# A fused attention, MoE and MoE kernel: seven block products in three quarters of the first MoE, one list planner for all work behind the attention, token operands in DRAM

## The chip, the cores and the metric

The kernel runs on one core of one Trainium2 chip. The metric is device time in microseconds (us) for one execution. A core has a TensorE (PE) that multiplies, a VectorE (DVE), a ScalarE (ACT) and a GpSimd (POOL) for everything else, and a SyncE (SP) whose queue issues the transfers. Each engine works through its own list of instructions in the order in which they were written, and waits at semaphores for the others. Matmuls write to PSUM, which has eight banks of 512 fp32 values per partition.

## The reference

```python
attn_out = _attn_ref(q, k, v)                     # 4 x 8 heads, 576 positions, banded masks
x = attn_out.transpose(0, 2, 1, 3).reshape(2304, 512)
# first MoE: d_ff = 2048
h = x @ w_in
g = np.maximum(h, 0.0) + alpha * np.minimum(h, 0.0)
x = g @ w_out
# second MoE: 8 experts of 1024, weighted by P (8 rounds of row and column normalising)
P = sinkhorn(x @ w_gate)
for e in range(8):
    out += P[:, e:e + 1] * (np.maximum(x @ w1[e], 0.0) @ w2[e])
```

## The kernel before, in words

Every product is computed from two fp32r parts of each operand, a high part and the rest: three matmuls (high x high, high x rest, rest x high) for each 128-row tile, written by the helper `three` (L362). So each operand must be split first: ACT copies the high part, and DVE or POOL subtracts it.

The program has three stages.

**Attention** (L164 to L353). Sixteen groups, each a pair of heads of one of four batches, go through five steps: scores `att_S`, exponentials `att_E`, sums `att_R`, transposes `att_X`, values `att_V`. `att_V` (L245) leaves 288 tokens at a time in `XS`, as the two parts (`xh`, `xl`). Between these steps stand units of the first MoE.

**First MoE.** A unit is a chunk of 288 tokens (eight of them, `NCH`) times a slice of 256 hidden columns (eight, `st`). `m1_L1` (L367) multiplies by `w_in`, applies the leaky relu and splits the result; `m1_L2` (L397) multiplies by `w_out` and adds to the accumulator `acc` of the chunk, on DVE (L413) or, for the first slice, by a copy on ACT (L411). The 64 units are written one behind another, the second layer of a unit merged with the first layer of the next (`run`, L578). Beside them `Side` objects hand out small pieces of other work at a rate set by a due step: the conversion of the weights, which come as 64-bit words and are turned into fp32 parts by `from_double` (L507, five instructions on DVE, then ACT and POOL), the attention (`aside`), the gate (`gside`), and the conversion of four w1 weight sets of the second MoE ahead of time (`pside`, `convert_ahead`, L642).

**Second MoE.** 768 tokens at a time (three blocks), sixteen half experts each, so 48 passes. Both layers use seven products of quarter blocks in place of eight (`PRODUCTS`, L733): sums of the blocks of both operands are formed first, and the results are put together from the seven products. In the first block some passes (`EIGHTH`, six of sixteen) use the plain eight products in the second layer. The order of all this work is made by a list planner, `arrange` (L804): each operation has a cost per engine and a due time, and at each step the engine that is free first takes its most urgent ready operation. The tail of the first MoE (`close_m1`, L949) goes through the planner as well.

PSUM in the second MoE: `W01` and `X01` of two banks each for the first layer, and `SW0`, `SW1`, `SX0`, `SX1` for the second.

Of the kernel before, what the change touches and what calls it, by code (L numbers as in the profile page):

```python
# [43 lines left out]
PRE = 4  # L44
EIGHTH = (0, 1, 4, 7, 10, 13)
# [14 lines left out]
def program(tc, qk, v, moe_w_in, moe_w_out, moe_alpha, moe2_w_gate, moe2_w1, moe2_w2, masks, out):  # L60
# [7 lines left out]
    spill = pool(es, "spill", space=bass.MemoryType.DRAM)  # L68
    py = pool(sp, "py", bufs=2, space=PSUM)
# [15 lines left out]
    gp = pool(sr, "gp", bufs=2, side="right")  # L85
    accp = pool(sr, "accp", side="right")
    attc = pool(sa, "attc", side="right")
# [4 lines left out]
    accs = [None] * 3 + [accp] * 3 + [None] * 2  # L92
# [9 lines left out]
    eye = attc.tile([P, P], BF16, name="eye")  # L102

# [141 lines left out]
    def att_V(i):  # L245
# [6 lines left out]
        for g in range(2):  # L252
            pv = bank("psV")
            for j in range(g * (NB // 2), NB // 2 + 1 + g * (NB // 2)):
                lo, hi = max(j * QB, g * CH), min((j + 1) * QB, (g + 1) * CH)
                for hh in range(2):
# [6 lines left out]
                    )  # L263
            if p < 2:
                c = 2 * b + g
                nc.scalar.copy(xh(c, p), pv[:, :CH])
                low_part(nc.vector, xl(c, p), pv[:, :CH], xh(c, p))
                continue
            for cc in range(2):
# [5 lines left out]
                low_part(nc.vector, lo, src, ho)  # L275

# [83 lines left out]
    below = [None]  # L360
# [6 lines left out]
    def m1_L1(n, c, st):  # L367
        ah, al = wa_of[n]
        for t in range(FS // P):
# [7 lines left out]
            gh = gp.tile([P, CH], F32R, tag="gh", name="gh", bufs=4)  # L377
            gl = gp.tile([P, CH], F32R, tag="gl", name="gl", bufs=4)
            u = gp.tile([P, CH], F32, tag="u", name="u")
            if below[0] is None:  # L380
                nc.vector.tensor_scalar(
                    out=u, in0=ps[:, :CH], scalar1=0.0, scalar2=alpha[:, ft : ft + 1], op0=ALU.min, op1=ALU.mult
                )
                nc.vector.scalar_tensor_tensor(out=u, in0=ps[:, :CH], scalar=0.0, in1=u, op0=ALU.max, op1=ALU.add)
            else:
                neg = below[0].tile([P, CH], F32, tag="neg", name="neg")
                nc.scalar.activation(neg, ps[:, :CH], AF.Relu, scale=-1.0)  # L387
                nc.vector.scalar_tensor_tensor(  # L388
                    out=u, in0=neg, scalar=rest[:, ft : ft + 1], in1=ps[:, :CH], op0=ALU.mult, op1=ALU.add
                )  # L390
# [56 lines left out]
    for st in order[2:-2]:  # L447
        add_units(inst_of(("a", st)), st, range(NCH), order)
    ends = [inst_of(("a", st)) for st in order[-2:]]
    for cs in ((0, 1), (2,), (3,), (4,), (5,), (6,), (7,)):  # L450
        for inst, st in zip(ends, order[-2:]):
            add_units(inst, st, cs, order)
# [1260 lines left out]
```

## Time and profile before

| | |
|---|---|
| median of 3 runs | 1971.38 us (1966.68 to 1973.65) |
| the profiled execution | 1972.87 us, its span 1971.1 us |
| PE busy | 1940.9 us, 98% of the span |
| DVE, ACT, POOL busy | 71%, 47%, 33% |
| granted TensorE clock, mean | 0.995 |
| moved by DMA | 408.34 MB, mean 207 GB/s |
| share of PE in the chain that ended last | 94% |

How to read it: a busy share is of the whole span, and a matmul's own duration contains its way through the array, so neighbouring matmuls overlap. What a matmul costs in a row of them is the distance from start to start. In the page's 40 slices PE stands at 9 (90% or more) in all but the first, and the clock in all of them. The times of the stages, from the trace: the first unit of the first MoE starts at 39.9 us, the last attention group ends in the unit that starts at 155.0, the second MoE's first product starts at 521.05.

### The profile page before, as it was taken

The page shows a single profiled execution, that of the slowest core. Times are in us where ns is not written, and L with a number is a line of the kernel's source. Part 1 is how long each engine was busy: PE and PEld are TensorE (multiplying, and loading weights), DVE is VectorE, ACT ScalarE, POOL GpSimd, SP SyncE. Part 2 cuts the span into 40 slices and gives each one's busy share as a digit, 9 for nine tenths or more (in the row PEclk, how much of TensorE's full clock was granted, in tenths as well). Part 3 has the DMA queues.
Part 4 walks back from the last instruction along what each step waited for, and adds up shares of the span by engine and source line. Part 5 has one row for each costly group of instructions (what it writes and reads, how often), then busy time and mean ns, then how long its engine had stood idle before and what let it go on. Part 6 is the DMA issues. An engine that isn't in the chain of part 4 may idle for free.

```text
span 1971.1 us, 37433 instructions
## 1 busy us (share of the span) xinstructions
PE 1940.9 (98%) x14755; PEld 1919.9 (97%) x14755; DVE 1409.0 (71%) x2302; ACT 928.4 (47%) x1740; POOL 644.2 (33%) x569
## 2 busy tenths in 40 slices
PE   6999999999999999999999999999999999999999
PEld 5889999999999999999999999999999999999998
DVE  6765776764458888777786777777776777777776
ACT  6654444434445555555545444444444443443442
POOL 4434666645235464545422332120200100100100
PEclk9999999999999999999999999999999999999999
DMA  7422343320457777666786886757687666766762
GB/s 236 142 76 70 115 144 121 131 86 29 141 177 256 277 260 278 233 218 248 262 342 233 310 304 216 254 195 241 231 307 274 237 217 215 240 214 215 242 212 86
DMA packets 126607, 408.34 MB, mean 207 GB/s; under 512 B 13024, under 2 KB 41440, under 8 KB 122080
## 3 DMA queue, kind: packets, MB, share of 16 engines
q1 hardware_dynamic: 126432, 405.95, 59.5%
q8 instruction: 116, 1.90, 0.4%
q14 instruction: 59, 0.48, 0.1%
HBM read 294.76 MB, written 111.15 MB: 206 GB/s over the span
## 4 chain that ended last, share of the span: by engine, by line
PE 94%; DMA 2%; DVE 1%; issue 1%; POOL 1%; ACT 1%; SPq 0%; POOLq 0%; DVEq 0%; ACTq 0%
PE SW L365 7%; PE SW L363 7%; PE SW L364 7%; PE W L363 7%; PE W L364 7%; PE W L365 7%; PE SX L365 6%; PE SX L364 5%; PE SX L363 5%; PE X L363 5%; PE X L364 5%; PE X L365 5%; PE psH L363 3%; PE psH L365 3%; PE psH L364 3%; PE psY L363 3%
## 5 line engine op out<-in xcount | busy, mean ns | idle before, releaser
L1499 DVE SCALAR_TENSOR_TENSOR oR<-SW,pt,oR 128x256 f32<-128x256 f32 x372 | 174.3, 480 | 125.4 <-PE SW L365 120.9
L363 PE MATMUL W<-XS,WT 128*128 128x384 f32 x768 | 258.4, 336 | 0.0
L364 PE MATMUL W<-XS,WT 128*128 128x384 f32 x768 | 257.8, 336 | 0.0
L365 PE MATMUL W<-XS,WT 128*128 128x384 f32 x768 | 257.6, 335 | 0.0
L1499 DVE SCALAR_TENSOR_TENSOR oR<-SX,pt,oR 128x256 f32<-128x256 f32 x360 | 171.9, 480 | 87.4 <-PE SX L365 86.9
L363 PE MATMUL X<-XS,WT 128*128 128x384 f32 x576 | 194.4, 338 | 2.8 <-ACT X L1343 2.8
L364 PE MATMUL X<-XS,WT 128*128 128x384 f32 x576 | 193.9, 337 | 0.0
L365 PE MATMUL X<-XS,WT 128*128 128x384 f32 x576 | 193.8, 337 | 0.0
L599 POOL TENSOR_TENSOR WT<-RAW,WT 128x512 fp32r<-128x512 f32 (+1 forms) x75 | 98.7, 1325 | 270.7 <-ACT WT L1167 136.8
L392 POOL TENSOR_TENSOR gl<-u,gh 128x288 fp32r<-128x288 f32 x126 | 104.1, 826 | 178.5 <-ACT gh L391 174.0
L364 PE MATMUL psH<-XS,WT 128*128 128x288 f32 x504 | 149.2, 296 | 1.3 <-DVE XS L143 1.3
L363 PE MATMUL psH<-XS,WT 128*128 128x288 f32 x504 | 150.3, 298 | 0.1
L365 PE MATMUL psH<-XS,WT 128*128 128x288 f32 x504 | 149.4, 296 | 0.0
L599 POOL TENSOR_TENSOR wR<-rawR,wR 128x512 fp32r<-128x512 f32 x38 | 51.0, 1342 | 300.3 <-ACT wR L1167 145.2
L363 PEld LDWEIGHTS W<-XS,WT 128*128 128x128 f32 x768 | 144.7, 188 | 0.2
L364 PEld LDWEIGHTS W<-XS,WT 128*128 128x128 f32 x768 | 144.4, 188 | 0.0
L365 PEld LDWEIGHTS W<-XS,WT 128*128 128x128 f32 x768 | 144.1, 188 | 0.0
L599 DVE TENSOR_TENSOR hR<-WX,hR 128x768 fp32r<-128x768 f32 x127 | 142.2, 1124 | 0.6 <-ACT hR L1289 0.3
L388 DVE SCALAR_TENSOR_TENSOR u<-neg,rest,psH 128x288 f32<-128x288 f32 x108 | 55.4, 513 | 114.0 <-ACT neg L387 107.4
L1289 ACT CAST hR<-WX 128x768 fp32r<-128x768 f32 x128 | 105.4, 835 | 65.0 <-DVE WX L1365 60.6
L599 POOL TENSOR_TENSOR WT<-rawR,WT 128x512 fp32r<-128x512 f32 (+1 forms) x47 | 63.5, 1357 | 168.4 <-ACT WT L1167 73.6
L363 PE MATMUL psY<-gh,WT 128*128 128x288 f32 x376 | 113.2, 301 | 1.0 <-ACT acc L411 1.0
(275 smaller groups left out, 6509.4 us busy)
## 6 DMA issues: line engine op xcount, KB each, us to landing
RAW<-in_moe_w SPq DMA_DIRECT2D x19, 1024.0 KB, 6.7
WT<-a11g SPq DMA_DIRECT2D x36, 512.0 KB, 4.4
WT<-S2g SPq DMA_DIRECT2D x36, 512.0 KB, 4.4
WT<-a12g SPq DMA_DIRECT2D x36, 512.0 KB, 3.6
WT<-S3g SPq DMA_DIRECT2D x36, 512.0 KB, 3.7
WT<-S1g SPq DMA_DIRECT2D x36, 512.0 KB, 3.6
WT<-a22g SPq DMA_DIRECT2D x36, 512.0 KB, 4.6
WT<-S4g SPq DMA_DIRECT2D x36, 512.0 KB, 4.0
```

Source lines behind the costliest of these rows:

```text
L363: nc.tensor.matmul(ps, lh, rh, start=start, stop=False, skip_group_check=more)
L364: nc.tensor.matmul(ps, lh, rl, start=False, stop=False, skip_group_check=more)
L365: nc.tensor.matmul(ps, ll, rh, start=False, stop=stop, skip_group_check=more)
L388: nc.vector.scalar_tensor_tensor(out=u, in0=neg, scalar=rest[:, ft : ft + 1], in1=ps[:, :CH], op0=ALU.mult, op1=ALU.add)
L392: nc.gpsimd.tensor_tensor(out=gl, in0=u, in1=f(gh), op=ALU.subtract)
L599: eng.tensor_tensor(out=out, in0=x, in1=y, op=op)
L1289: add(act(n2), lambda _: nc.scalar.copy(hv(h[n])[:, 0], tm[i]), prio, [("t", i)], [(h[n], "h")])
L1499: nc.vector.scalar_tensor_tensor(out=o, in0=x, scalar=p_, in1=o, op0=ALU.mult, op1=ALU.add)
```

## The change

**First MoE.** Only the first two slices (`st` 0 and 1, a quarter of d_ff) keep the plain form. The other six are taken as three blocks of 512 hidden columns, and each block is computed for one batch (576 tokens) at a time: twelve passes. Their first layer uses the seven products; the second layer stays plain, twelve matmuls for each output tile. The leaky relu works on 576 columns at once (`leaky`).

**Accumulators.** In the new second layer each output tile is seeded: ACT copies the accumulator into the PSUM bank before the matmuls add to it, and copies the sum back after them. DVE's additions of L413 are gone there.

**Token operands.** `att_V` also copies each value tile, unsplit, to `xst`, and SP stores it to DRAM (`x32`). From there `m1_tokens` loads a batch, forms the four sums on DVE or POOL, splits them and stores them to DRAM (`xm`). Later passes load their operands from there.

**Weights.** Eight pieces of the first new block's weights are converted during the attention stage (`early`) and stored to DRAM (`wd`); the other sixteen are converted between the new passes (`double`).

**Planner.** From the tenth unit on (the first one on chunk 6) everything is ordered by `arrange`: seven plain units, twelve new passes, 48 passes of the second MoE. A place in SBUF now has a plan of uses by era. Of w1 only one set is converted ahead (`AHEAD`), and the first block has seven passes with eight second-layer products: `EIGHTH` is (0, 1, 2, 5, 8, 11, 14).

```diff
-PRE = 4
-EIGHTH = (0, 1, 4, 7, 10, 13)
+EIGHTH = (0, 1, 2, 5, 8, 11, 14)
...
+    x32 = [spill.tile([P, KD, 2 * CH], F32, name=f"x32b{b}") for b in range(B)]
...
+            if g == 0:
+                whole = xst[:, i % 2]
             if p < 2:
                 c = 2 * b + g
                 nc.scalar.copy(xh(c, p), pv[:, :CH])
+                nc.scalar.copy(whole[:, g * CH : (g + 1) * CH], pv[:, :CH])
                 low_part(nc.vector, xl(c, p), pv[:, :CH], xh(c, p))
+                if g:
+                    nc.sync.dma_start(x32[b][:, p], whole)
                 continue
...
+    def early(i):
+        load_raw(piece_at[2, i])
+        yield from from_double(raw_of.pop((2, i)), None, None, wd[i])
+        load_raw(piece_at[2, i] + 2)
...
+        if far is not None:
+            nc.gpsimd.tensor_tensor(out=ab, in0=t, in1=lw, op=ALU.add)
+            nc.sync.dma_start(far, ab)
+            return
...
+        def m1_layer1(v):
+            fi = 1 + v // B
...
+            for i, (a, xn, bk) in enumerate(PRODUCTS):
+                ps = WX01[bk]
...
+                        for k in range(2):
+                            three(ps[:, st, :CH], wv[:, 0, k, st], wv[:, 1, k, st], x[:, 0, k], x[:, 1, k], first and k == 0, k == 1, True)
...
+        def m1_layer2(v):
...
+            for cc in range(2):
+                c = 2 * b + cc
+                for d in range(KD):
+                    K, bk = next_bank(4 if v < B else 3)
...
+                    if seeded:
+                        add(act(CH), lambda _, c=c, d=d, bk=bk: nc.scalar.copy(bk[:, :CH], acc[c][:, d]), t - 1, [A], [K])
+                    add([("PE", 1.59)], mm, t, reads, [K])
+                    if seeded:
+                        add(act(CH, True), lambda _, c=c, d=d, bk=bk: nc.scalar.copy(acc[c][:, d], bk[:, :CH]), t + 1.2, [K], [A])
...
-        for i, u in enumerate(units[:-1]):
+        hand = next(i for i, u in enumerate(units) if u[2] == NCH - 2)
+        EARLY_AT = 4
+        for i, u in enumerate(units[:hand]):
+            if i == EARLY_AT:
+                for j in range(EARLY):
+                    wside.add(early(j), 5, begin[hand - 1])
...
+        second(prev, units[hand:])
```

**Matmuls.** Up to the start of the tenth unit PE's list is the same in both kernels, row for row. Over the whole program it has 3136 matmuls of 288 columns before and 2992 after, 6156 of 256 columns before and 6174 after, and as many of every other width.

**DVE, from the second hidden values of the eighth unit on** (`u`, `GU`: hidden values; `XS`: values of the attention; L531 before and L522 to L536 now: steps of a weight conversion). Before:

```order
L381 TENSOR_SCALAR u<-psH,alpha 128x288
L384 SCALAR_TENSOR_TENSOR u<-psH,u 128x288
L143 TENSOR_TENSOR XS<-psV,XS 128x2x72 x8
L531 SCALAR_TENSOR_TENSOR RAW<-RAW 128x512
L381 TENSOR_SCALAR u<-psH,alpha 128x288
L384 SCALAR_TENSOR_TENSOR u<-psH,u 128x288
L413 TENSOR_TENSOR acc_96<-psY,acc_96 128x288
```

Now:

```order
L396 TENSOR_SCALAR GU<-psH,alpha 128x288
L399 SCALAR_TENSOR_TENSOR GU<-psH,GU 128x288
L146 TENSOR_TENSOR XS<-psV,XS 128x2x72 x4
L532 TENSOR_SCALAR RAW<-WX 128x512
L536 SCALAR_TENSOR_TENSOR RAW<-RAW 128x512
L522 TENSOR_SCALAR WX<-RAW 128x512
L146 TENSOR_TENSOR XS<-psV,XS 128x2x72 x4
L526 SCALAR_TENSOR_TENSOR WX<-RAW,WX 128x512
L530 SCALAR_TENSOR_TENSOR WX<-WX 128x512
L532 TENSOR_SCALAR RAW<-WX 128x512
L536 SCALAR_TENSOR_TENSOR RAW<-RAW 128x512
L522 TENSOR_SCALAR WX<-RAW 128x512
```

The first hidden values of the ninth unit, the fifth row before, now come four rows behind the last one shown (the rest of the conversion that it begins). One step of a conversion stood ahead of them; now the last two steps of one and two whole ones do. From the fifth unit's second hidden values to this place the list now holds eight conversions, before parts of two.

**SP, the same stretch** (`RAW`: two buffers for weight words; `wd`: converted pieces). Before:

```order
L476 DMA RAW<-in_moe_w_in 128x1024
L129 DMA v<-in_v 96x1152
L476 DMA RAW<-in_moe_w_in 128x1024
L129 DMA v<-in_v 96x1152 x2
L648 DMA praw<-in_moe_w 128x4x256
L660 DMA a11g_2358<-pboth 256x1x256
L476 DMA RAW<-in_moe_w_out 128x1024
```

Now:

```order
L542 DMA wd_108<-WX 128x512
L485 DMA RAW<-in_moe_w_out 128x1024
L275 DMA x32b_63<-xst 128x576
L287 DMA x32b_63<-xst 128x576
L132 DMA v<-in_v 96x1152
L542 DMA wd_109<-WX 128x512
L485 DMA RAW<-in_moe_w_out 128x1024
L542 DMA wd_110<-WX 128x512
L485 DMA RAW<-in_moe_w_out 128x1024
L287 DMA x32b_63<-xst 128x576 x2
L542 DMA wd_111<-WX 128x512
```

Each load into a RAW buffer stands behind the store of a converted piece and behind the stores of the tokens, which wait for ACT.

**ACT, first MoE in its steady part.** Before:

```order
L537 CAST WT<-WX 128x512
L654 CAST pboth<-praw 128x256
L387 ACTIVATE neg<-psH 128x288
L391 CAST gh<-u 128x288
L517 ACTIVATE WX<-RAW 128x512
```

Now:

```order
L1284 ACTIVATE WX<-X_2340 128x576
L1358 COPY acc_102<-SX_2343 128x288
L1355 COPY SX_2343<-acc_102 128x288
L1286 CAST XS<-WX 128x576 x2
L1284 ACTIVATE WX<-W_2339 128x576
L1358 COPY acc_102<-SX_2344 128x288
```

Each bank of the second layer (`SX`, `SW`) is now copied back and seeded again by two neighbouring rows, between the copies of the first layer.

## Rows read from the trace of the kernel before

**Rows 1.** The page, part 1: busy time, share of the span, instructions

```profile
PE 1940.9 (98%) x14755; PEld 1919.9 (97%) x14755; DVE 1409.0 (71%) x2302; ACT 928.4 (47%) x1740; POOL 644.2 (33%) x569
```

**Rows 2.** Busy us by stretch: PE, PEld, DVE, ACT, POOL; clock; DMA; GB/s

```profile
300.00:350.00 50.00, 50.00 (x379) 50.00 (x378) 34.66 (x71) 21.01 (x51) 34.04 (x41) 1.00 0.37 121
600.00:650.00 50.00, 50.00 (x362) 49.93 (x362) 40.61 (x64) 28.25 (x44) 24.39 (x18) 1.00 0.73 259
```

**Rows 3.** Timeline of PE: start, duration, instruction; seven rows between

```profile
1100.05 0.29 PE L363 MATMUL SX<-WT,hR 128*128 128x256 f32 x1
...
1101.01 0.28 PE L365 MATMUL SW<-wR,hR 128*128 128x256 f32 x1
```

**Rows 4.** The same, two stretches of the attention stage

```profile
39.90:77.40 37.50, 32.47 (x460) 28.38 (x458) 25.95 (x56) 25.54 (x93) 16.33 (x13) 0.95 0.41 126
115.10:155.00 39.90, 35.30 (x382) 32.65 (x379) 23.98 (x54) 20.12 (x57) 12.36 (x12) 0.91 0.24 74
```

**Rows 5.** Timeline of DVE, two instructions, others between

```profile
112.94 1.12 DVE L197 TENSOR_REDUCE mx<-psS 128x5 f32<-128x480 f32 x2 [0.57 <-PE psS L186]
...
156.90 0.52 DVE L381 TENSOR_SCALAR u<-psH,alpha 128x288 f32<-128x288 f32 x1 [1.39 <-PE psH L365]
```

**Rows 6.** Groups by line, a weight conversion: busy us, mean ns, idle before

```profile
L518 DVE TENSOR_SCALAR WX<-RAW 128x512 uint32<-128x512 uint32 x7 | 3.2, 459 | 6.9 <-DMA RAW<-in_moe_w_in 6.9
L522 DVE SCALAR_TENSOR_TENSOR WX<-RAW,WX 128x512 uint32<-128x512 uint32 x7 | 4.8, 679 | 0.1
L525 DVE SCALAR_TENSOR_TENSOR WX<-WX 128x512 f32<-128x512 f32 x9 | 9.1, 1015 | 0.9
L527 DVE TENSOR_SCALAR RAW<-WX 128x512 uint32<-128x512 uint32 x7 | 2.9, 421 | 0.1
L531 DVE SCALAR_TENSOR_TENSOR RAW<-RAW 128x512 f32<-128x512 uint32 x7 | 5.0, 721 | 0.1
L542 POOL TENSOR_TENSOR WX<-WX,WT 128x512 f32<-128x512 f32 x9 | 12.9, 1428 | 19.9 <-DVE RAW L527 11.0 <-ACT WT L529 6.6 <-DVE rest L113 2.3
```

**Rows 7.** DMA issues, us to landing: 0 to 170, then 100 to 161

```profile
RAW<-in_moe_w_in SPq DMA_DIRECT2D x6, 512.0 KB, 5.3
...
RAW<-in_moe_w_in SPq DMA_DIRECT2D x2, 512.0 KB, 3.2
```

**Rows 8.** Timelines of DVE and of POOL, one instruction each

```profile
100.73 1.94 DVE L525 SCALAR_TENSOR_TENSOR WX<-WX 128x512 f32<-128x512 f32 x1
...
100.16 1.96 POOL L222 TENSOR_TENSOR s<-s,rs 128x864 f32<-128x864 f32 x1 [1.76 <-DVE rs L221]
```

**Rows 9.** Groups by line on ACT

```profile
L411 ACT COPY acc<-psY 128x288 f32<-128x288 f32 x32 | 13.0, 418 | 2.4 <-PE psY L365 2.4
L391 ACT CAST gh<-u 128x288 fp32r<-128x288 f32 x126 | 54.6, 434 | 111.4 <-DVE u L388 77.9 <-DVE u L384 31.9 <-POOL s L222 1.6
L1343 ACT COPY X<-W 128x768 f32<-128x768 f32 x48 | 37.6, 784 | 17.1 <-PE W L365 16.9
L595 ACT CAST gxh<-acc 128x576 fp32r<-128x576 f32 x12 | 7.8, 669 | 0.0
L1167 ACT CAST WT<-RAW 128x512 fp32r<-128x512 f32 x103 | 62.3, 620 | 47.0 <-DMA RAW<-in_moe_w 13.4 <-PE W L364 12.5 <-PE SW L365 3.6
```

**Rows 10.** The hand-over to the second MoE: busy time by stretch and PE's waits

```profile
515.00:540.00 25.00, 22.42 (x142) 21.55 (x141) 10.44 (x18) 10.37 (x19) 2.84 (x3) 0.93 0.64 224
...
PE X L363 <- ACT X L1343: 2.6, 1, 2.6
```

**Rows 11.** Groups by line on DVE in the second MoE

```profile
L599 DVE TENSOR_TENSOR hR<-WX,hR 128x768 fp32r<-128x768 f32 x127 | 142.2, 1124 | 0.6 <-ACT hR L1289 0.3
L1365 DVE SCALAR_TENSOR_TENSOR WX<-W,WX 128x768 f32<-128x768 f32 x84 | 76.4, 951 | 19.1 <-PE W L365 19.1
L1499 DVE SCALAR_TENSOR_TENSOR oR<-SW,pt,oR 128x256 f32<-128x256 f32 x372 | 174.3, 480 | 125.4 <-PE SW L365 120.9 <-issue 1.9 <-DMA out<-oR 0.9
L1424 DVE SCALAR_TENSOR_TENSOR oR<-SX,pt,oR 128x512 f32<-128x512 f32 x12 | 9.0, 748 | 2.8 <-PE SX L365 2.5
```

More of the change, by code (lines that the diff above doesn't have):

```diff
@@ L376, in m1_L1 @@
             ft = st * (FS // P) + t
[L377 to L390, printed above, removed]
+            k = made[0]
+            made[0] += 1
+            gh, gl = gview(k % 4)
+            u = GU[:, k % 2]
+            nc.vector.tensor_scalar(
+                out=u, in0=ps[:, :CH], scalar1=0.0, scalar2=alpha[:, ft : ft + 1], op0=ALU.min, op1=ALU.mult
+            )
+            nc.vector.scalar_tensor_tensor(out=u, in0=ps[:, :CH], scalar=0.0, in1=u, op0=ALU.max, op1=ALU.add)
             nc.scalar.copy(gh, u)
@@ L670, in program @@
-    lgs = {}
-    gate_split = set()
-    def gate(c, parts):
-        flush()
-        ps = bank("psG")
-        gate_mm(ps, parts)
-        gate_out(c, ps)
-    def gate_mm(ps, parts):
-        for kk in range(KD):
-            for i in range(2):
-                nc.tensor.matmul(
-                    ps[: 2 * E, :CH],
-                    wg[:, kk],
-                    parts[kk // 2][i][:, kk % 2],
-                    start=(kk == 0 and i == 0),
-                    stop=(kk == KD - 1 and i == 1),
-                )
@@ L807, in add @@
         return o
+    arranging = []
     def arrange(places, more):
-        free = {c: list(v) for c, v in places.items()}
+        free = {c: [] for c in queue_of}
         heads = {c: 0 for c in queue_of}
@@ L817, in arrange @@
         wire = [0.0]
+        BACKLOG, FAR = 5.0, 30.0
         done = []
@@ L856, in arrange @@
                 continue
-            lead = max(o.engines.values()) + (5.1 if "SP" in o.engines else 0.1)
+            cost = max(o.engines.values())
+            lead = cost * 1 + 0.1 + (5 if "SP" in o.engines else 0)
             o.prio = min(x.prio for x in o.next) - lead
-        for c in queue_of:
-            bind(c)
+        for place in places:
+            admit(place, 0.0)
         while len(done) < len(ops):
@@ L869, in arrange @@
             t, e = best
-            o = min((o for o in lists[e] if at(o, e) <= t), key=lambda o: (o.prio, o.seq))
+            o = min((o for o in lists[e] if at(o, e) <= t), key=lambda o: (o.prio + (5 if e == "DVE" and "POOL" in o.engines else 0), o.seq))
+            if e == "SP" and wire[0] > t + BACKLOG and o.prio > t + FAR:
+                o.ready = wire[0] - BACKLOG
+                continue
             cost = o.engines[e]
@@ L883, in arrange @@
             done.append(o)
-            for c, ats in more.get(o, {}).items():
-                free[c] += [(end, at) for at in ats]
-                bind(c)
+            for place in more.get(o, ()):
+                admit(place, end)
             late = end + (0.25 if e == "PE" else 0.1)
@@ new lines, in second, with release @@
+        g_done = joined_many(4, lambda: g_next)
+        g_next = [right_place(words_of(GP, 4 * CH * j, 4 * CH), [("h", 2), ("w2", NF - 1)]) for j in range(2)]
+        g_places = [Place(lambda k=k: gview(k), [("g", ALL)], g_done) for k in range(4)]
+        places += g_places[2:]
+        d_done = joined(2, Place(words_of(RAW, 0, 2048), [("raw", ALL)]))
+        places += [Place(words_of(RAW, 1024 * i, 1024), [("dbl", ALL)], d_done) for i in range(2)]
+        def release(keys, prio, freed):
+            add([("PE", 0.0)], lambda _: None, prio, (), keys)
+            later_places[ops[-1]] = freed
@@ L1132, in weights @@
             b = got[m, u] = {}
-            full = (m == 1 or g >= PRE) and sb_ == (m if plain2(g) else 0)
+            full = (m == 1 or not any(g in x for x in AHEAD.values())) and sb_ == (m if plain2(g) else 0)
             plain, sums = PLAIN[m], {s[0]: s[1:] for s in SUMS[m]}
```

977 lines of the change are left out of this document (658 added, 319 removed).

## The prediction

> **What bounds the kernel now.** First the page's busy times: PE 98% of the span, DVE 71%, ACT 47%, POOL 33% [rows 1]. A busy PE may still be a slow one, so second the busy time by stretch, with the number of matmuls. In a steady stretch of the first MoE PE is busy 50.00 of 50 us, the clock is full, and 379 matmuls of 288 columns take 50 us: 0.132 us each, start to start. In the second MoE it is busy 50.00 of 50 as well [rows 2], and there a row of eight 256-column matmuls takes 0.96 us, 0.120 each [rows 3]. So behind the attention PE is bound by the number of its matmuls, and a matmul less is worth its distance in full. In the attention stage this is not so: from 39.9 to 77.4 PE is busy 32.47 of 37.5 us, from 115.1 to 155.0 it is busy 35.30 of 39.9 with a clock of 0.91, and there PE waits for chains through the other engines [rows 4]. A change that takes matmuls out of the later part and puts DVE and ACT work into the attention stage therefore has to be weighed in two places.
>
> **Step 1: the matmuls.** A new pass has 7 x 12 = 84 matmuls in its first layer where eight products would have 96: 12 less, in 12 passes 144, as the two lists say (3136 - 2992). 144 x 0.132 = 19.0 us less [rows 2]. One more pass of the second MoE has eight products in its second layer: 18 matmuls of 256 columns more, 18 x 0.120 = 2.2 us [rows 3]. Both stand on PE's own list, which is full there, so nothing of them is hidden: -16.8 us.
>
> **Step 2: eight early conversions on DVE.** One conversion is five DVE instructions of 459, 679, 1015, 421 and 721 ns, 3.3 us, and a POOL addition of 1.43 us [rows 6]. The eight must be through before the ninth unit's first hidden values, which DVE takes up at 156.90 now; the list before them begins at the maxima of 112.94 [rows 5]. So the stretch is 44.0 us long. DVE works 23.98 of 39.9 us in its middle [rows 4]; without the parts of two conversions in it, about 6 us, some 18 are left, and with the ends of the stretch some 20. The conversion ahead of it is also finished earlier in the new list, which puts 2.7 us more in front. 20 + 2.7 + 8 x 3.3 = 49 us of DVE work for 44 us: at best 5 us late. Worse, there are only two RAW buffers: a conversion's buffer is refilled when POOL has read it (1.43), and the load takes 3.2 to 5.3 us to land [rows 7]; with some 0.5 us for hand-overs a buffer is back 5.1 to 7.2 us after its conversion. The other buffer's conversion with its share of other work takes 3.3 + 20/8 = 5.8. At 5.3 us a pair costs 5.8 + 7.2 = 13.0, and as the first two pieces are there already, eight cost 3 x 13.0 + 11.6 = 50.6, with the 2.7 us in front 53.3 us for 44: 9.4 late. And DVE cannot be full: of the 15.9 us that it is idle there, some are waits for PE and ACT that stay. I take 10 us, a little over the slow landing. The ends: 5 us if it packs perfectly; 26 us if nothing of 8 x 3.3 finds an idle place. What is behind: the second layer of the eighth unit and the first planned unit need the PSUM banks that DVE empties, so PE waits for all of it.
>
> **Step 3: 32 copies on ACT and their stores.** A 288-column copy from PSUM takes 418 ns [rows 9], 32 x 0.418 = 13.4 us. From 77 to 115 us PE is full and hides them; from 115 on they are beside the DVE queue of step 2. Where they can show is the early stretch, in which PE has 5.0 us of waits and ACT is busy 25.54 of 37.5 [rows 4]: eight copies, 3.3 us at most, 0 at least. I take 1.5. SP issues 16 stores among the loads; a store waits for ACT's copy, and the next `v` and `qk` loads behind it with it, which is in the same bound.
>
> **Step 4: the new passes themselves.** PE needs 180 x 0.132 = 23.8 us for one. ACT's own work in a pass: three copies and four relus of 576 columns from PSUM (between 418 for 288 and 784 for 768, so 0.62 us), four casts of 669, eight seeds (no such row; nearest 434, a copy of 288 out of SBUF) and eight copies back of 418 [rows 9]: 4.3 + 2.7 + 3.5 + 3.3 = 13.8 us. From ACT's list 37 weight casts of 620, 25 token and gate casts of 669, 16 first conversion steps of about as much and a few others fall into these twelve passes: 58 us, 4.8 a pass. That is 18.6 of 23.8 us, 78%. An engine so full beside a full PE is not new here: DVE is busy 40.61 of 50 us while PE misses nothing [rows 2], and that is the same planner. I take 0. Its cover is the other two second-layer banks; what it costs without cover is the slow rival below. Seeds could be dearer than their nearest row; at 784 ns each, the row for 768 columns, they add 2.8 us to a pass and it still fits (21.4). The store and reload of the tokens adds transfers to a stretch in which DMA is busy 0.37 [rows 2]; the second MoE's stretch runs at 0.73 with a full PE, so I take 0 for these too.
>
> **Step 5: the hand-overs.** Before, PE waits 2.6 us for one ACT copy at the start of the second MoE, and the clock over these 25 us is 0.93 of full, so 7% or 1.7 us are lost to the half level after this stop [rows 10]: 4.3 us. Now the second MoE's first products stand among second-layer tiles of the last new pass, so most of this goes. But the first new pass runs nearly alone: its products go to only two pairs of banks in turn, and the third, fifth and seventh wait for what ACT and DVE do with the first, third and fifth (a copy of 0.62, then two or three DVE steps of 0.5 to 0.8). I take 3 us for it, between 0 and 6. Net -1.
>
> **Step 6: the second MoE's first block.** Three w1 sets are now converted there: 3 x 7 casts on ACT and 3 x 11 additions that DVE would do in 0.8 us, 26 us. The extra eight-product pass spares four low parts of 1124, three joins of 951 and more on the first layer, and 18 x 480 against 6 x 748 on the second [rows 11], about 12 us, and puts off the sums for its w2. Over four passes (120 us) DVE goes from 81% to some 90%. I take 0, with 5 us as the far end.
>
> **The sum.** -16.8 + 10 + 1.5 + 0 - 1 + 0 = -6.3 us. Against the profiled execution, 1972.87, that is 1966.6; this one lies 1.5 us above the median of the runs, so I give it against the median: 1971.38 - 6.3 = 1965 us. The forecast's own range, with 5 to 15 us for step 2, is 1960 to 1970. What a measurement of this kernel can tell from no change is about 0.3%, 5.9 us, so the forecast lies just at this edge.
>
> **Rivals.**
> *DVE packs well.* If the loads land in 3.2 us and the attention's waits fall on the conversions, step 2 costs its 5 us or less, step 3 nothing: -16.8 + 4 - 1 = -13.8, 1957.5 us. For it: DVE is idle 15.9 of 39.9 us there [rows 4]. Against: DVE's work has to stand in a fixed order behind loads.
>
> *DVE and POOL in each other's way.* The same DVE step that takes 0.69 us elsewhere took 1.94 while POOL ran a 1.96 us multiplication of two SBUF operands [rows 8]. Eight more POOL additions of two SBUF operands lie beside 24 DVE steps that read two. If every conversion loses these 1.25 us once, 10 us more: -6.3 + 10 = +3.7, 1975 us, no change that can be told. The Trainium skill (GPSIMD Engine Reference, section Specifications) has such a rule: GpSimd shares its SBUF interfaces with VectorE, and they contend when a VectorE instruction has two SBUF inputs; the rows of 1.94 and 1.96 us agree, though eight of nine such steps before show nothing of it.
>
> *ACT's queue sets the pace of the new passes.* Place: seed and copy back of the second layer's three banks. A bank comes round every 3/8 of 23.8 = 8.9 us; its tile takes 1.6, copy back and seed 0.85, so PE waits once ACT's queue is over 6.4 us late, about ten casts. For it: 78% on one queue in fixed order, with the costs of seeds unseen so far. Against: DVE at 81% without a gap [rows 2]. If it decides, a wait of about 1.2 us in each of twelve passes, 14.4 us: -6.3 + 14.4 = +8.1, 1979.5 us, slower.
>
> *The products are not saved:* the lists of matmuls exclude it.
>
> **How the numbers follow.** Forecast 0.47, DVE packs well 0.20, DVE and POOL 0.13, ACT 0.17, anything else 0.03. Faster by over 0.3% (below 1965.5) is the second and somewhat over half of the forecast: 0.47. Slower by as much (above 1977.3) is ACT's rival, a small part of the third and the rest: 0.21. The same: 0.32. The range takes in the three rivals, 1957.5 to 1979.5, with little around them: 1955 to 1980.
>
> **What would show it.** After: 2992 matmuls of 288 columns and, between 200 and 450 us, the same 0.132 us between them (step 1). The ninth unit's hidden values at about 167 us and the first planned unit's matmuls (W) 10 us later than the tenth unit's were, with PE waiting on DVE there, and DVE near full from 115 to 167 (step 2). ACT busy near 78% in the new passes with PE's waits for ACT under 1 us a pass (step 4). No 2.6 us wait before the second MoE (step 5). It is wrong if the attention stage is longer by under 5 or over 15 us, or if PE in the new passes waits for seeds.

## The result, and the profile after

The changed kernel takes 1992.18 us (median of four runs, 1987.26 to 1994.85), the kernel before 1971.70 beside it. The ratio is 1.0105, 95% interval 1.0078 to 1.0132: slower by one per cent, and outside my range. The profiled execution has a span of 1990.9 us.

The page, part 1 (busy us, share, instructions), to be set against [rows 1]. PE has 126 instruction records fewer and the same busy time:

```profile
PE 1939.9 (97%) x14629; PEld 1912.9 (96%) x14629; DVE 1449.8 (73%) x2223; ACT 1031.5 (52%) x1915; POOL 549.7 (28%) x413
```

PE's list up to the start of the tenth unit is the same in both kernels, so a place in it can be looked up in both traces. The tenth unit's first matmul on its list, called the **first planned matmul** from here on, stands in PE's timeline (start, duration, instruction) of the kernel before at

```profile
161.41 0.30 PE L363 MATMUL psH<-XS,WT 128*128 128x288 f32 x1
```

and after at

```profile
190.43 0.40 PE L378 MATMUL W<-XS,WT 128*128 128x288 f32 x1 [0.55 <-DVE acc L422]
```

The attention stage lost 29.0 us. From there to the end of the span it is 1809.7 us before (1971.1 - 161.4) and 1800.5 after (1990.9 - 190.4): the rest gained 9.2 us. 29.0 - 9.2 = 19.8, the difference of the spans.

**Where in the attention stage.** Busy time by stretch (PE with count, PEld, DVE, ACT, POOL; clock; DMA share; GB/s), cut at the same places of PE's list. Before, the stretches that [rows 4] do not have:

```profile
0.00:39.90 39.90, 27.29 (x424) 21.96 (x424) 26.81 (x55) 26.29 (x105) 16.96 (x19) 0.96 0.84 267
77.40:115.10 37.70, 37.70 (x496) 34.73 (x492) 30.61 (x61) 26.06 (x80) 17.25 (x14) 1.00 0.40 122
155.00:161.40 6.40, 6.40 (x50) 6.40 (x49) 3.65 (x8) 1.27 (x3) 1.31 (x2) 1.00 0.01 3
```

After:

```profile
0.00:47.90 47.90, 31.90 (x425) 25.44 (x425) 27.37 (x56) 29.25 (x113) 16.63 (x19) 0.79 0.74 256
47.90:85.70 37.80, 32.44 (x460) 28.34 (x458) 25.95 (x56) 27.46 (x100) 16.31 (x13) 0.95 0.53 169
85.70:127.60 41.90, 38.56 (x497) 34.90 (x493) 34.01 (x65) 28.52 (x87) 20.72 (x16) 1.00 0.52 165
127.60:178.30 50.70, 41.58 (x378) 37.49 (x379) 41.56 (x76) 26.53 (x73) 19.92 (x16) 0.81 0.49 156
178.30:190.40 12.10, 8.82 (x49) 8.24 (x48) 7.96 (x16) 1.94 (x4) 4.19 (x4) 0.80 0.46 161
```

The losses are 8.0, 0.3, 4.2, 10.8 and 5.7 us. The first has no early conversion in it, the fourth most of them: there DVE is busy 41.56 us, 17.6 more than in the same piece of work before. PE stops there, and behind its stops the mean granted clock is 0.81 where it was 0.91, so part of this stretch ran at the lower of the clock's two levels (1.2 GHz in place of 2.4): on the chain of waits matmuls of 288 columns stand 0.24 us apart there, 0.13 at the full clock. The first stretch has the same at 0.79 (0.96 before).

**What ended the waits.** PE's longest (waited for: us in total, times, longest), 0 to 80, 110 to 195 and 195 to 285 us:

```profile
PE psV L260 <- DMA v<-in_v: 5.7, 2, 4.6
...
PE psY L378 <- DVE GU L399: 5.5, 3, 2.8
...
PE SW L379 <- DVE XS L593: 4.4, 1, 4.4
```

The first was the surprise: PE waits 4.6 us for a load of `v`. SP's queue tells why. Its waits from 0 to 200 us, in the same columns:

```profile
SPq L542 <- POOL WX L541: 32.4, 6, 7.5
...
SPq L287 <- ACT xst L284: 26.8, 4, 11.2
SPq L287 <- DMA x32b<-xst: 19.8, 8, 4.0
```

Its token stores in the same time (count, KB each, us to landing):

```profile
x32b<-xst SPq DMA_DIRECT2D x24, 288.0 KB, 2.3
```

There are 24 token stores, not the 16 that I had counted. For the first two pairs of a batch (`p < 2`) the store inside the loop, L275, runs, and then the one behind the loop, L287, stores the same tile again. The second must wait until the first has landed, and the next `v` load stands behind it. So the stores hold the queue twice over: 26.8 us in four waits for ACT's copy, 19.8 us in eight for a landing. SP's timeline:

```profile
33.48 0.33 SPq L275 DMA_DIRECT2D x32b<-xst  x1
37.84 0.33 SPq L287 DMA_DIRECT2D x32b<-xst  x1
38.26 0.39 SPq L132 DMA_DIRECT2D v<-in_v  x1
```

The 4.6 us are not the whole early loss of 8.0: the 40 matmuls `psV` right behind the wait took 2.40 us, the 40 before it 1.39, so the lower clock took part of the rest.

**The conversions.** Three pieces of the chain of waits between 100 and 195 us, 13.3 us together, are loads into the two RAW buffers, and some conversion steps on it last nearly three times as long as others of their kind, 0.69 to 0.70 us (start, us):

```profile
122.24 1.95 DVE WX L530
139.72 2.02 DVE WX L526
155.70 3.44 DMA RAW<-in_moe_w_out
161.37 4.98 DMA RAW<-in_moe_w_out
177.54 4.88 DMA RAW<-in_moe_w_out
```

**Behind the attention.** Four stretches, columns as above:

```profile
200.00:215.00 15.00, 15.00 (x115) 15.00 (x115) 4.35 (x9) 7.97 (x21) 0.81 (x1) 1.00 1.00 366
245.00:260.00 15.00, 9.54 (x62) 8.63 (x61) 13.18 (x18) 7.74 (x13) 7.68 (x5) 0.94 0.67 264
300.00:350.00 50.00, 50.00 (x378) 50.00 (x377) 44.04 (x72) 37.23 (x76) 19.14 (x15) 1.00 0.38 124
850.00:900.00 50.00, 47.63 (x335) 46.71 (x334) 41.03 (x59) 25.57 (x43) 24.29 (x17) 1.00 0.62 232
```

The new passes run as forecast: 378 matmuls in 50.00 us, as in [rows 2], ACT busy 37.23, no gap. The first new pass stops: from 245 to 260 PE works 9.54 of 15 us. Just before, from 200 to 215, DVE had been idle for 10.65 of 15 us while the DMA was full. I also summed, over the matmuls of a stretch, the distance from start to start beyond its usual value. Against the kernel before that makes 8 us more from 200 to 300 (the first new pass), 4.3 less from 500 to 550 (the old hand-over, [rows 10]), and 5 more from 550 to 1150 (the second MoE's first block). With the 16.8 us of matmuls: -16.8 + 8 - 4.3 + 5 = -8.1, near the 9.2 found above.

### The profile page after: what moved, and what is told of

It reads as the page before. It is cut to its first block, busy times and chain, and to the rows that moved or that the text cites. A ratio compares the mean times of both kernels' runs of the same rounds, so it can differ in the third digit from the quotient of the medians.

```text
span 1990.9 us, 36935 instructions
## 1 busy us (share of the span) xinstructions
PE 1939.9 (97%) x14629; PEld 1912.9 (96%) x14629; DVE 1449.8 (73%) x2223; ACT 1031.5 (52%) x1915; POOL 549.7 (28%) x413
## 4 chain that ended last, share of the span: by engine, by line
PE 91%; DVE 4%; DMA 2%; ACT 1%; issue 0%; SPq 0%; DVEq 0%; ACTq 0%
PE W L378 8%; PE W L380 8%; PE W L379 8%; PE SW L380 8%; PE SW L379 8%; PE SW L378 8%; PE SX L380 7%; PE SX L378 7%; PE SX L379 7%; PE X L380 6%; PE X L378 6%; PE X L379 6%; PE psS L189 1%; DMA RAW<-in_moe_w_out 1%; PE psV L260 1%; DMA v<-in_v 1%
## 5 line engine op out<-in xcount | busy, mean ns | idle before, releaser
L378 PE MATMUL W<-XS,WT 128*128 128x384 f32 (+1 forms) x936 | 308.2, 329 | 1.5 <-DVE acc L422 0.6
L380 PE MATMUL W<-XS,WT 128*128 128x384 f32 (+1 forms) x936 | 307.2, 328 | 1.3 <-DVE WT L593 1.3
L379 PE MATMUL W<-XS,WT 128*128 128x384 f32 (+1 forms) x936 | 307.3, 328 | 0.0
L1889 DVE SCALAR_TENSOR_TENSOR oR<-SW,pt,oR 128x256 f32<-128x256 f32 x363 | 170.0, 479 | 121.3 <-PE SW L380 119.6
L380 PE MATMUL X<-XS,WT 128*128 128x384 f32 (+1 forms) x660 | 218.4, 331 | 0.8 <-DVE WT L593 0.8
L378 PE MATMUL X<-XS,WT 128*128 128x384 f32 (+1 forms) x660 | 218.6, 331 | 0.0
L379 PE MATMUL X<-XS,WT 128*128 128x384 f32 (+1 forms) x660 | 218.2, 331 | 0.0
L378 PEld LDWEIGHTS W<-XS,WT 128*128 128x128 f32 x936 | 176.2, 188 | 2.7 <-DVE acc L422 0.9
L380 PEld LDWEIGHTS W<-XS,WT 128*128 128x128 f32 x936 | 175.7, 188 | 1.6 <-DVE WT L593 1.6
L379 PEld LDWEIGHTS W<-XS,WT 128*128 128x128 f32 x936 | 175.9, 188 | 0.0
L593 POOL TENSOR_TENSOR WT<-rawR,WT 128x512 fp32r<-128x512 f32 (+1 forms) x60 | 79.6, 1332 | 251.5 <-ACT WT L1555 165.5
L593 POOL TENSOR_TENSOR WT<-RAW,WT 128x512 fp32r<-128x512 f32 (+1 forms) x57 | 78.0, 1370 | 257.2 <-ACT WT L1555 113.5
L593 DVE TENSOR_TENSOR XS<-WX,XS 128x768 fp32r<-128x768 f32 (+1 forms) x117 | 122.5, 1048 | 18.6 <-ACT XS L1286 18.3
L380 PEld LDWEIGHTS X<-XS,WT 128*128 128x128 f32 x660 | 123.9, 188 | 1.7 <-DVE WT L593 1.5
L378 PEld LDWEIGHTS X<-XS,WT 128*128 128x128 f32 x660 | 124.1, 188 | 0.2
L379 PEld LDWEIGHTS X<-XS,WT 128*128 128x128 f32 x660 | 124.0, 188 | 0.0
L1745 ACT ACTIVATE WX<-WX 128x768 f32<-128x768 f32 x48 | 40.6, 847 | 155.1 <-DVE WX L593 155.1
L593 POOL TENSOR_TENSOR wR<-RAW,wR 128x512 fp32r<-128x512 f32 x39 | 52.6, 1351 | 243.8 <-ACT wR L1555 156.7
```

The source lines that it names most:

```text
L378: nc.tensor.matmul(ps, lh, rh, start=start, stop=False, skip_group_check=more)
L379: nc.tensor.matmul(ps, lh, rl, start=False, stop=False, skip_group_check=more)
L380: nc.tensor.matmul(ps, ll, rh, start=False, stop=stop, skip_group_check=more)
L593: eng.tensor_tensor(out=out, in0=x, in1=y, op=op)
L1745: add(act(n2), lambda _: nc.scalar.activation(tm[1], tm[1], AF.Relu), t + 1, [("t", 1)], [("t", 1)])
L1889: nc.vector.scalar_tensor_tensor(out=o, in0=x, scalar=p_, in1=o, op0=ALU.mult, op1=ALU.add)
```

## The experiments

Theories for the attention stage: **Q**, SP's queue, in which the token stores hold up the loads behind them; **R**, the cycle of the two RAW buffers through DVE, POOL and a load; **W**, the sheer number of DVE and ACT steps; **C**, DVE steps made longer by POOL's operations. For the first new pass: **L**, the order of the transfers ahead of it. All runs, the kernel before beside them at 1969.5 to 1971.7 us:

| kernel | first planned matmul | from there to the end | median us | ratio to before, 95% |
|---|---|---|---|---|
| changed kernel | 190.4 | 1800.5 | 1992.18 | 1.0105 (1.0078 to 1.0132) |
| one_store | 182.2 | 1801.3 | 1985.55 | 1.0079 (1.0064 to 1.0094) |
| ahead | 183.7 | 1802.2 | 1987.22 | 1.0087 (1.0070 to 1.0104) |
| both | 179.8 | 1800.8 | 1982.68 | 1.0063 (1.0048 to 1.0079) |
| no_conv | 172.4 | 1800.9 | 1973.33 | 1.0015 (1.0006 to 1.0025) |
| no_tokens | 173.8 | 1800.7 | 1978.62 | 1.0050 (1.0031 to 1.0069) |
| late | 185.7 | 1799.2 | 1985.69 | 1.0080 (1.0067 to 1.0094) |
| all3 | 181.2 | 1797.0 | 1978.35 | 1.0042 (1.0029 to 1.0055) |
| all3_four | 168.7 | 1799.4 | 1969.95 | 1.0000 (0.9991 to 1.0008) |
| no_add | 180.9 | 1796.7 | 1975.41 | 1.0037 (1.0023 to 1.0050) |
| no_copies | 164.2 | 1798.5 | 1964.62 | 0.9980 (0.9971 to 0.9989) |
| sbuf_four | 169.3 | 1798.6 | 1969.65 | 0.9999 (0.9990 to 1.0008) |
| direct_four | 164.1 | 1799.2 | 1965.79 | 0.9976 (0.9966 to 0.9986) |

The scatter first: `late` has the same attention code as the changed kernel, and its first planned matmul still came 4.7 us earlier. So a shift of less than 5 us in one profile proves nothing. The medians scatter too: the four runs of the changed kernel span 7.6 us, and `late`, whose edit the third column puts at 1.3 us, has a median 6.5 us lower. A gain of this size against the changed kernel is rough; between two of the edited kernels, whose runs mostly lie closer together, it says more. The third column is steadier: in the six kernels with the same planned lists it lies between 1800.5 and 1802.2.

**one_store**: the second store goes.

```diff
-        nc.sync.dma_start(x32[b][:, p], whole)
+        if p >= 2:
+            nc.sync.dma_start(x32[b][:, p], whole)
```

> The changed kernel stores the tokens of the first two pairs of a batch twice: the line in the loop and the line behind it both run, and SP's queue waits at the second store until the first has landed (19.8 us over eight such waits). Here the second one is left out; the values are the same. Theory Q (SP's queue holds the loads of v and of the weight words behind those stores): the 4.6 us wait of PE for v near 38 us goes, the weight words come earlier, the first planned matmul moves from 190.4 us to 180 to 184, the whole to 1982 to 1986 us. Theory R (the loss after 115 us is the cycle of the weight words' two buffers through DVE and POOL): only the wait for v goes, first planned matmul at 185 to 187, 1987 to 1989 us. Theory W (it is the sheer work of the eight conversions on DVE and ACT): the same 1987 to 1989.

Measured: 1985.55, 6.6 us less, with 182.2. The wait for `v` is gone; the load is issued right behind the store (SP's timeline):

```profile
32.67 0.33 SPq L275 DMA_DIRECT2D x32b<-xst  x1
33.09 0.38 SPq L132 DMA_DIRECT2D v<-in_v  x1
```

This is the result Q named, though the numbers of R and W lie only 1.5 to 3 us off, inside the scatter. What the trace shows beyond it is that the wait is gone. Against `ahead`, `both` is 4.5 us lower by the same edit, so the double store costs a quarter to a third of the whole loss of 20 us.

**ahead**: the last DVE step writes beside the sum, and the load goes first.

```diff
+        if far is not None:
+            lw = ab
         nc.vector.scalar_tensor_tensor(
             out=lw, in0=low, scalar=2.0**-52, in1=pw.bitcast(F32), op0=ALU.mult, op1=ALU.mult
         )
+        if far is not None:
+            load_raw(then)
         yield
```

> In the eight early conversions the last DVE step writes its result beside the sum instead of back into the buffer of the weight words, so that POOL's addition no longer reads that buffer, and the next load is issued right behind that DVE step, ahead of POOL's addition and of the store of the piece. Values are the same. Theory R (the cycle of the two buffers; 13 us of the chain to the first planned matmul are loads of weight words): 8 to 13 us less, first planned matmul at 177 to 182, 1979 to 1984 us. Theory Q (SP's queue held by the token stores): under 3 us less, since the loads still stand behind those stores. Theory W (work on DVE and ACT): under 3 us less.

Measured: 1987.22, 5.0 us less, where R had 8 to 13 and the others under 3. Against `one_store`, `both` is 2.9 us lower by the same edit. The loads have left the chain of waits, and DVE steps stand there in their place. R's cycle is on the chain, but at 2.9 to 5.0 us it is worth less than half of my price, and the bound of the others is not clearly passed.

**no_conv** and **no_tokens** leave out one side each.

```diff
-        yield from from_double(raw_of.pop((2, i)), None, None, wd[i])
+        raw_of.pop((2, i))
...
+        nc.sync.dma_start(wd[i], moe2_w1[i // 4, :, i % 4])
```

> Leaves out the work of the eight early conversions on ACT, DVE and POOL: the weight words are still loaded, and the stored pieces are filled by transfers from another input, so the weights of the first new block are not the model's. Theories R and W (both lay the loss after 115 us on these conversions): the first planned matmul at 166 to 172 us, 1966 to 1974 us, that is 18 to 25 us less. Theory Q: 8 us less at the most, 1984 us or above.

Measured: 1973.33, 18.9 us less, first planned matmul at 172.4, at the upper end of what R and W had, and 11.0 us above the kernel before that are not the conversions'.

```diff
-                nc.scalar.copy(whole[:, g * CH : (g + 1) * CH], pv[:, :CH])
...
-        nc.sync.dma_start(x32[b][:, p], whole)
+        if p == 3:
+            nc.sync.dma_start(x32[b], qk[b, :, :, 0].rearrange("p r c -> r p c"))
```

> Leaves out the 32 copies of the unsplit tokens and their 24 stores; the token buffer in DRAM is filled by one transfer a batch from another input, so the four sums of the new passes are not formed from the model's tokens. Theory Q: the whole early loss of 8 us goes (first hidden matmul back at 40 us from 47.9), and the later one shrinks with it, first planned matmul at 172 to 178, 1974 to 1980 us. Theories R and W: the early 8 us go, what is lost after 115 us stays (about 20 us), first planned matmul at 181 to 184, 1983 to 1986 us.

Measured: 1978.62, 13.6 us less, first planned matmul at 173.8, in Q's range; the early 8 us are gone wholly (the first hidden matmul at 38.9 us). The two leave-outs together move that matmul by 18.0 + 16.6 = 34.6 us where only 29.0 were lost. The 5.6 us over are hardly more than the scatter of single profiles, so it is not shown that a part of the loss belongs to both, say the RAW loads that stand behind token stores.

**both**: the edits of one_store and ahead together.

> Both edits together: one store of the tokens, and the load of weight words ahead of POOL's addition. If the two remove different waits (one the wait for v and the late issue of loads, the other the cycle through POOL), their gains add: first planned matmul at 190.4 - 8.2 - 6.8 = 175.4 us and 1980 to 1982 us. If they shorten the same cycle of loads, the second adds little: 180 to 182 us, 1984 to 1986 us. If what is left is DVE's work, slowed beside POOL (10 us of lengthened steps between 112 and 184 us with the loads ahead), the first planned matmul doesn't come below 174 us whatever the loads do.

Measured: 1982.68, 9.5 us less than the changed kernel, between the two forecasts (6.6 + 5.0 = 11.6 would be additive). The first planned matmul stays above 174, as the third sentence had it.

**late**: one due time in the planner.

```diff
-                    release([("xs", b, n)], 0, [strip_place(b, n)])
+                    release([("xs", b, n)], sF(v + 1), [strip_place(b, n)])
```

The release of the value tiles was due at 0, and the planner hands that urgency to what must come before it: twelve stores of 576 KB (`b11b` and so on, 187 to 203 us). The loads of the tokens and of the converted weights stood behind them.

> The changed kernel with one number of the planner changed: the release of the attention's value tiles is due at the end of each batch's first pass and not at time 0, so that the loads of the tokens and of the converted weights go ahead of the twelve 576 KB stores (187 to 203 us) that stand before them now. Theory L (the 4.4 us wait at 253 us and the clock behind it come from DVE work that starts 17 us late, behind those stores, while DVE stands idle 10 of 15 us from 200 to 215): first planned matmul unchanged at 190 us, the wait gone or under 1 us, 4 to 8 us less, 1984 to 1988 us. Rival P (DVE's work ahead of the first new pass is too much in any order): the wait stays, within 2 us of 1992.

Measured: 1985.69, 6.5 us less, but 4.7 us of this is the scatter named above. By the third column the edit is worth 1.3 us here, no more than that column's own spread, and 3.8 between `both` and `all3`. The loads are now issued at 183.65 (203.55 before the edit), and DVE works where it was idle (13.56 us instead of 4.35):

```profile
200.00:215.00 15.00, 14.89 (x112) 14.65 (x111) 13.56 (x19) 10.29 (x27) 6.35 (x4) 1.00 0.63 246
```

PE's wait falls from 4.4 to 2.2 us, not under 1, and it is now for a step on POOL. L holds in part. That the rest is P's, too much work ahead of the first new pass in any order, fits but is not shown.

**all3**: the three edits.

> The three edits together. If each acts at its own place: 1992.2 - 6.6 - 5.0 - 6 = 1974 to 1976 us, still a little slower than before, with the first planned matmul at 175 to 177 us and no wait over 1 us in the first new pass. If the first two overlap: 1978 to 1980 us.

Measured: 1978.35, 13.8 us less than the changed kernel: the second forecast, with the first two edits overlapping. PE still waits 2.2 us once in the first new pass, where the forecast had no wait over 1. 8 us above the kernel before are left.

**all3_four**: `EARLY = 4` on top.

> The three edits, and only the four pieces of w_in are converted in the attention stage; the four of w_out are converted by the planner's own list behind it. Theory W (what is left after 115 us is DVE's work with its slowed steps): half of it goes, first planned matmul at 167 to 171 us, and if DVE's idle time between 190 and 230 us takes the four conversions, 1966 to 1970 us, below the kernel before. Rival: they land on the first new pass, where DVE is busy 60.6 of 70 us, and the wait there comes back: 1974 to 1980 us.

Measured: 1969.95, level with the kernel before and not below it. Four conversions fewer bring the first planned matmul from 181.2 to 168.7, 3.1 us for each, about what one needs on DVE (3.3, [rows 6]), as if no part of the second four had found an idle place. The planner takes them for 2.4 us more (third column); the rival's wait comes back, 4.2 us of PE in two pieces, but not at the rival's price.

**no_add**: `all3` without POOL's eight additions.

```diff
-            nc.gpsimd.tensor_tensor(out=ab, in0=t, in1=lw, op=ALU.add)
-            nc.sync.dma_start(far, ab)
+            nc.sync.dma_start(far, t)
```

> The kernel with the three edits, without POOL's eight additions at the end of the early conversions: the low words are left out of those eight pieces of the weights (a relative change below a millionth), DVE and ACT do all that they did. Theory C (DVE steps that read and write SBUF alone last as long as POOL's neighbouring operation; 10.5 us of lengthened steps between 112 and 184 us): the lengthened part falls to 4 to 7 us, the first planned matmul from 181.2 us to 176 to 179, 1973 to 1976 us. Theory W (only the number of DVE steps counts): first planned matmul within 1.5 us of 181.2 and 1977 to 1979 us.

The groups of three conversion steps (busy us, mean ns, idle before), 112 to 181 us, `all3` and then `no_add`:

```profile
L526 DVE SCALAR_TENSOR_TENSOR WX<-RAW,WX 128x512 uint32<-128x512 uint32 x9 | 9.9, 1098 | 0.1
L530 DVE SCALAR_TENSOR_TENSOR WX<-WX 128x512 f32<-128x512 f32 x9 | 8.8, 983 | 0.9
L522 DVE TENSOR_SCALAR WX<-RAW 128x512 uint32<-128x512 uint32 x9 | 6.5, 725 | 0.0
```

```profile
L530 DVE SCALAR_TENSOR_TENSOR WX<-WX 128x512 f32<-128x512 f32 x9 | 8.4, 929 | 0.9
L526 DVE SCALAR_TENSOR_TENSOR WX<-RAW,WX 128x512 uint32<-128x512 uint32 x9 | 8.0, 884 | 0.1
L522 DVE TENSOR_SCALAR WX<-RAW 128x512 uint32<-128x512 uint32 x9 | 4.5, 501 | 3.6 <-DMA wd<-WX 3.6
```

Taken against 680 (L526), 690 (L530) and 390 ns (L522), about what they need undisturbed, these steps are lengthened by 9.4 us with the additions and by 5.0 without: C's mechanism is shown. What it is worth at the end is not. The profile has the first planned matmul still at 180.9, as W said, but it is of the slowest of the five runs (1979.34); three others took 1974.67 to 1975.41, as C said, and less than any run of `all3` (1977.33 to 1979.98). My edit made a wait of its own, since the store now holds the buffer that the next conversion writes first (3.6 us in the last row).

**no_copies**: `all3_four` without ACT's 32 copies.

> The kernel with the three edits and four early pieces, without ACT's 32 copies of the unsplit tokens: the 16 stores stay, and store a constant, so the four sums of the new passes are not formed from the model's tokens. If ACT's copies, which also hold the PSUM bank of the values, make the remaining early loss (4.1 us behind the kernel before at the unit of 79 us): it falls to between -3 and 0 us, first planned matmul from 168.7 to 163 to 166, 1965 to 1968 us. If SP's stores make it: the early loss stays at 3 to 5 us and the time at 1969 to 1971.

Measured: 1964.62, first planned matmul at 164.2, 0.6 us behind the kernel before at the unit of 79 us (the forecast had 0 at most): ACT's copies make it. The stores are still there, but they no longer wait for a copy, so the loads behind them could have made it too. By PE's waits they did not: up to 95 us PE waits 10.0 us for loads in `all3_four` and 11.3 here, and 8.9 and 6.1 us for ACT and DVE.

**sbuf_four**: `all3_four`, with the values copied out of PSUM once and split from that copy.

```diff
+        nc.scalar.copy(hi, src)
+        low_part(nc.vector, lo, src, hi)
```

> The kernel with the three edits and four early pieces, and the values of the attention leave PSUM once: ACT copies them unsplit, and the high part (one cast of 576 columns a group) and the rest (one DVE step of 576) are formed from that copy. ACT then does 16 x (2 copies + 1 cast) in place of 16 x (2 or 4 casts + 2 copies), DVE 16 steps in place of 48. If the price of the copies is ACT's time and the hold on the PSUM bank: the early loss of 4.1 us goes, first planned matmul at 162 to 166 us, 1963 to 1967 us, faster than the kernel before. Rival C: the DVE step now reads two SBUF operands and is held beside POOL's operations, up to 1.3 us at each of 16, and the values come later to the first MoE: 1968 to 1974 us.

Measured: 1969.65, a miss. The early loss shrank from 4.1 to 2.4 us, but from 118 us to the first planned matmul this kernel loses 5.5 us to the kernel before, all3_four only 2.8, a difference that lies inside the scatter of single profiles. The rival took little of it: of the 16 new DVE steps, 0.76 us undisturbed, four are lengthened, by 1.6 us together and by 0.5 behind 118 us. What else took it stays open.

**direct_four**: `all3_four` without copies and stores; the planner adds the two parts up again.

```diff
+            for i, n in ((1, "b12"), (0, "b11"), (3, "b22"), (2, "b21")):
+                part, keys = (lambda h, n=n: xs_view(b, n)[:, h]), [("xs", b, n)]
...
+                add(flex(n2), lambda e, i=i, part=part: sub(E3[e], blk(i), f(part(0)), f(part(1)), ALU.add), prio, keys, [(r, i)])
```

> No unsplit copies and no token stores in the attention stage at all: behind it the planner adds the two parts of each block again (four DVE or POOL additions of 576 columns a batch) and forms the four sums from that; only one block of three batches, both parts, goes through DRAM. Four early pieces, the early release of RAW and the later release of the value tiles as before. If the tokens' copies and stores make the early loss and the planner hides sixteen additions: first planned matmul at 162 to 166 us (no_copies had 164.2) and 1962 to 1967 us, faster than the kernel before by 0.2 to 0.4%. Rival: in front of the first new pass DVE has no room for four more additions (3.1 us), and the wait there grows by as much: 1967 to 1971 us, no change.

Measured: 1965.79, ratio 0.9976 (0.9966 to 0.9986): a little faster than the kernel before, and 26 us faster than the changed one. Its stages, at the same places of PE's list as above:

```profile
40.40:78.00 37.60, 32.60 (x463) 28.21 (x459) 26.01 (x57) 25.60 (x93) 16.33 (x13) 0.95 0.40 122
78.00:115.70 37.70, 37.70 (x494) 34.74 (x492) 31.05 (x59) 25.25 (x77) 17.33 (x14) 1.00 0.46 137
115.70:157.10 41.40, 34.61 (x383) 31.33 (x380) 32.68 (x66) 21.36 (x61) 17.56 (x14) 0.96 0.29 89
```

The early loss is 0.5 us. Four conversions raise DVE from 23.98 [rows 4] to 32.68 us in the third stretch and cost 1.5 us there: with this much idle time left, they nearly hide. In the first new pass PE waits 3.6 us once, about what the rival had, and the time is the first forecast's all the same.

## Why the prediction was wrong

**Step 1, the matmuls: right.** 2992 matmuls of 288 columns, and 378 in 50.00 us. The 16.8 us are gained; less than that arrives because steps 5 and 6 give part of it back.

**Step 2, eight conversions, "I take 10": mechanism right, size wrong.** It is worth 18.0 us at the first planned matmul and 18.9 on the whole (no_conv), inside my ends of 5 and 26 and far from the middle. The cycle of load, DVE and POOL was on the chain, as the step had it. What I left out of the sum: the loads stand on SP behind token stores, and the DVE steps themselves are lengthened. What each of the two cost is not shown.

**Step 3, copies and stores, "1.5, 3.3 us at most": this is the step that failed.** 11.0 us of the loss are left without any early conversion, and leaving the tokens out is worth 13.6. Three terms were wrong. "SP issues 16 stores" should read 24, which the code shows: `continue` leaves the inner loop only, so the last line runs for every group. I then put the stores' wait into the copies' bound, as if a load behind a waiting store waited no longer than ACT's copy; SP stands 26.8 us in four waits at L287 until ACT's copy is done, which itself waits for PE, and 19.8 us in eight for a landing. And a copy was priced by a row for contiguous columns, 418 ns [rows 9]. Half of the copies write with a stride (ACT's groups, after):

```profile
L284 ACT COPY xst<-psV 128x288 f32<-128x288 f32 x16 | 11.9, 745 | 0.0
L272 ACT COPY xst<-psV 128x288 f32<-128x288 f32 x16 | 7.1, 445 | 0.0
```

That is 19.0 us, not 13.4. DVE's low parts stand behind the strided copies (14.6 us of DVE's idle time in 13 waits for L284), and the PSUM bank of the values comes free only when both are done.

**Step 4, the new passes at 0: right**, ACT at 74% beside a full PE.

**Step 5, hand-overs, -1 net: wrong.** The old stop went, 4.3 us, as forecast. The first new pass cost 8 us instead of 3, and mostly not because of its banks: of PE's 6.2 us of waits there 4.4 are for one DVE result. The planner had put twelve large stores ahead of the loads that DVE needed, which explains a part: `late` was worth 1.3 to 3.8 us. The rows of SP's order that I chose to look at were those of the attention stage.

**Step 6, the second MoE at 0: at its far end.** About 5 us. From 850 to 900 us PE does 335 matmuls where the kernel before does 359. No run isolates the cause.

In the forecast's own terms: -16.8 + 29.0 (steps 2 and 3) + 3.7 (step 5) + 5 (step 6) = +20.9, where +20.5 was measured. For steps 2 and 3 the forecast had 11.5.

**The rivals.** *DVE packs well* did not happen: from 127.6 to 178.3 us DVE was busy 41.56 of 50.7 us, and the eight conversions cost 18. *DVE and POOL in each other's way* is real: the steps of [rows 8] come back, 9.4 us of lengthening in all3, close to the 10 of its price, though how much of it reaches the end is not shown. But I drew it as an alternative to the forecast at 1975 us, while it acts together with the waits of steps 2 and 3. And I misread its rows: of the nine such steps before, three were lengthened (1.93, 1.11 and 1.94 us) and not one. They are the three that began while a POOL operation was running; the other six had none beside them. The Trainium skill (SBUF — State Buffer, section SBUF: two separate sides) is sharper than the rule that I cited: of two instructions that need it, the one that starts first holds the shared pair of ports to its end, and the other engine's blocks. The trace agrees: after, between 112 and 190 us, 20 conversion steps on DVE overlap a POOL operation. Ten of them began while it ran, and nine of these are lengthened by more than 0.15 us; ten were under way when it began, and none of these is. Here is a lengthened one (DVE, then POOL):

```profile
122.24 1.94 DVE L530 SCALAR_TENSOR_TENSOR WX<-WX 128x512 f32<-128x512 f32 x1
```

```profile
121.67 1.96 POOL L225 TENSOR_TENSOR s<-s,rs 128x864 f32<-128x864 f32 x1 [0.36 <-DVE rs L224]
```

POOL ends at 123.63, and the DVE step 0.55 us later, which is near its own 0.69. *ACT's queue sets the pace* did not happen. None of the rivals named SP, the queue that every load of the stage passes through, and so none reached 1992: all of them moved one term while the others stayed at their middles. In fact steps 2, 3, 5 and 6 went to the dear side together. Steps 2, 3 and 5 share DVE and SP; for step 6 that is not shown.

## What to carry to other kernels

When a change adds stores to a queue that also issues loads, count the stores in the queue's list, and price each load behind them with the store's producer and, for a repeated target, with its landing. Where several added pieces of work share one engine or queue, add their bounds before choosing a middle: eight conversions cost 18 us where four, in `direct_four`, nearly hid. When a planner takes its urgency from successors, a release due at 0 makes everything before it urgent; look at the order of transfers at each hand-over.

## What the runs showed of the hardware

An ACT copy of 128x288 from PSUM took 445 ns when it wrote contiguous columns and 745 when it wrote with a stride. The DVE steps `XS<-psV`, which read one operand from PSUM, were not lengthened beside POOL: of 20 between 112 and 190 us nine overlap a POOL operation, six of these began while it ran, and none is longer. A step with one SBUF input was: L522, 0.42 to 0.43 us with no POOL operation beside it, lasted 1.50 at 166.44 beside POOL's operations from 165.70 on. Four other L522 steps that were under way when POOL's operation began kept their length. The lengthened one:

```profile
166.44 1.50 DVE L522 TENSOR_SCALAR WX<-RAW 128x512 uint32<-128x512 uint32 x1 [0.27 <-DMA RAW<-in_moe_w_out]
```
